# A new table of places for the preparations, and a plan with two transfer queues, in a planned attention and feed-forward kernel

## The chip, the cores and the metric

The kernel runs on one core of a Trainium2 chip. The metric is device microseconds (us) of one execution; lower is better. The kernel before was timed three times: median 1328.38 us, from 1326.26 to 1328.97. A core has five engines with their own instruction streams: PE (matrix products), DVE (VectorE), ACT (ScalarE), POOL (GpSimd) and SP (SyncE, which here only starts transfers).

## The reference

Attention over four batches, with keys that are means over 4 x 4 windows, and behind it a feed-forward layer with the activation h - tanh(h):

```python
kv_pool = kv.reshape(B, H // r, r, W // r, r, C).mean(axis=(2, 4))
k = v = kv_pool.reshape(B, -1, C) @ w_sr           # 768 keys of 128 per batch
a = softmax(q @ k.T / sqrt(C))                     # 12288 queries per batch
x = (a @ v).reshape(B * S, 128)
h = x @ w_in                                       # 128 -> 2048
out = (h - tanh(h)) @ w_out                        # 2048 -> 128
```

## The kernel before, in words

The 49152 queries are cut into 96 units of 512 (24 per batch). The kernel uses that the softmax is nearly flat and that x hardly moves about a centre: it computes exp(s) - 1 - s beside a straight (linear) term, and the feed-forward as a polynomial about the centre. A last part checks that this holds, and a branch that isn't taken here holds the general way.

One unit is, on each engine, a fixed row of work:

- PE: 3 pairs of score products (`scores`, L774), 3 pairs of value products (`values`, L818), 2 products for the softmax's sum (`shares`, L802), 2 x 3 straight products (L808, L878), 8 pairs into the wide layer (`forth`, L889) and 8 pairs back (`back`, L927). A product has 512 columns; a pair fills one of three PSUM tiles named `big`, or adds to the bank `acc`.
- ACT: 3 `exps` (L778), 7 `square` (L893), 1 `copy` (L900), and `result` (L938, tile o) that ends a unit and waits for the unit's last product into acc.
- DVE: 3 `beyond` (L781, tile r2, which `order` prints as r_ and a number), 7 `cube` (L896), 1 `apart` (L829, tile df).
- POOL: one of the eight wide tiles whole: `moved_pool` (L903, z), `times` (L907) twice (z, then rp, which the last product of the unit needs), the roundings `rounded` (L832, dr, from df; all `forth` of the unit need it), `lower_left` (L858, dl) and `lower_q` (L812, ql), and two accumulating transfers `added` (L797) that sum the three r2 tiles into rs for `shares`.
- SP: the transfers of q, of the first r2 tile into rs (`copied`, L794), and of the output.

Before the units of batch 1, 2 and 3, each batch has **preparations**, which run between the units of the batch before it: 15 accumulating transfers `gather` (L366, POOL; the 16th, the first, from SP) that sum the 16 places of a window into kvp; `keys` (L355: six partial sums L428, their mean L432 and L433, the centre L440 on PE, keys L447, values L456, moment L473), and `about_centre` (L504: the centre through the wide layer L536, small polynomial chains on POOL L561 to L592, scaled weights L636, L678, L698 on POOL, slopes L685 on PE). Batch 0's preparations run before the first unit; so do the weights' (`words_of`, `weights`), but for the product W W^T (L333), which only the last check needs.

The order is written by `Plan.run`: every piece of work has a step (its due place), an engine, a length and how late its result is, and the planner takes at each moment the piece that can start first, and among those within 0.1 us the one with the lowest step. The pieces of the units (`lane=True`) keep the order of their steps on each engine, which the table `AT` gives; the preparations are set between them by step. Each engine then runs its instructions in exactly that order, and waits at each for what it needs. A transfer costs the planner the time `dma` on one shared resource.

Of the kernel before, what the change touches and what calls it, by code (L numbers as in the profile page):

```python
# [22 lines left out]
KB = 64  # L23
# [23 lines left out]
class Plan:  # L47

    HOP = 0
    OWN = {"DVE": 0.16, "ACT": 0.02}  # L50
    SOON = 0.1

# [29 lines left out]
    def run(self, between):  # L82
# [25 lines left out]
        free, ready, done, begun, order = {}, {}, [0.0] * n, [0.0] * n, []  # L108
# [3 lines left out]
        while any(ready.values()):  # L112
            best = None
            for e, q in ready.items():
                if q:
# [6 lines left out]
                    if best is None or (start, step, i) < best[:3]:  # L122
                        best = start, step, i, e, r
            now, _, i, e, r = best
            ready[e].remove((r, i))
            step, _, us, _, late, port, dma = self.ops[i]
            free[e] = now + us
            if dma:
# [4 lines left out]
            begun[i], done[i] = now, now + us + late  # L133
            order.append((now, i))
            for k in then[i]:
                left[k] -= 1
                if not left[k]:
                    f = self.ops[k][1]
                    own = self.OWN.get(f, 0.0)
                    r = [done[j] + (self.HOP if self.ops[j][1] != f else own) for j in need[k]]  # L140
                    r = max(r + [begun[j] + 0.01 for j in behind[k]])
                    ready.setdefault(f, []).append((r, k))
# [14 lines left out]
def attention_then_ffn(ctx: ExitStack, tc: tile.TileContext, q, kv_by_key, kv_by_place, w_sr, w_in,  # L157
# [18 lines left out]

    DIRECT, HELD = 2, 6
# [3 lines left out]
            "most": 1}  # L181

# [51 lines left out]
    def words_of(step, load_step, n, kind):  # L234
# [55 lines left out]
        Y, M, part = (ym, "y"), (ym, "m"), (key, n)  # L290
        plan.op(load_step, "SP", 0.5, load_words, () if kind == "i" else ("held",), (words,), late=2.0,
# [13 lines left out]
    def weights(step, load_step):  # L305
# [3 lines left out]
        for j in range(2):  # L309
            turned = f"turned.{j}"  # L310
            big(turned, step + NW + j)
            for k in range(2):
# [6 lines left out]
                plan.op(step + NW + j, "PE", 1.0, turn, (("win32", 2 * j + k), "ident"),  # L319
# [5 lines left out]
            plan.op(step + NW + j, "ACT", 1.03, copy, (turned,), (("winT", j),), late=0.1)  # L325
        s = 16.0
        bank("WW", "x", s)
        sb("WW32", "W2", [P, P])
        bank("W4", "x", s + 1)
# [11 lines left out]
        norm(s + 1, "WW32", "W4", B)  # L341
# [13 lines left out]
    def keys(b, s0):  # L355
# [6 lines left out]
        NK = K // KB  # L362
        for w in range(W if b else 0):
            def gather(w=w):
                if w:
                    PL.dma_start(out=plan[kvp], in_=kv_by_place[b - 1, w], accum_op=ALU.add)  # L366
                else:
                    SP.dma_start(out=plan[kvp], in_=kv_by_place[b - 1, w])

            at = (b * NG - GATHER[b - 1] + max(w - 1, 0)) * UN + AT["more"][0] - 2 * UN  # L370
            plan.op(at - (0.01 if w else 4), *(("POOL", 0.87) if w else ("SP", 0.5)), gather, (), (kvp,),
                    late=3.0, dma=1.0, lane=w > 0)
        for j in range(0 if b else NK):
# [3 lines left out]
            at = slice(j * KB, (j + 1) * KB)  # L377

            def load(at=at, key=key):
                SP.dma_start(out=plan[key], in_=kv_by_key[:, at, :])  # L380

            plan.op(s - 8, "SP", 0.5, load, (), (key,), late=2.0, dma=1.27)
            if j % 3 == 2:
                for k, w in enumerate((8, 4, 2, 1)):
                    def fold(key=key, w=w, at=at):
                        x = plan[key]
                        to = plan[kvp][:, at].unsqueeze(2) if w == 1 else x[:, :, 0:w]
                        PL.tensor_tensor(out=to, in0=x[:, :, 0:w], in1=x[:, :, w : 2 * w], op=ALU.add)
# [3 lines left out]
            else:  # L392
                def pool(key=key, at=at):
                    V.tensor_reduce(out=plan[kvp][:, at], in_=plan[key], op=ALU.add, axis=AX.X)
# [13 lines left out]
        for x, at in ((pc, s0), (pm, s3), (p4, s4)):  # L408
            bank(x, "x", at)
# [74 lines left out]
        for n in range(NK // 2):  # L484
            of = (kvp,) if b else ((kvp, 2 * n), (kvp, 2 * n + 1))
            plan.op(s0 - 0.5, "DVE", 0.3, partial(part, n), of, ((row, n),))
        plan.op(s0, "DVE", 0.35, mean, (row,), (row,))
        plan.op(s0, "ACT", 0.85, apart, (kvp, row), (kvp,), late=0.1)
        plan.op(s0, "PE", 0.2, centre, ("wsr", row), (pc,), late=0.2)
        plan.op(s0, "DVE", 0.12, copy_centre, (pc,), (cen,))  # L490
# [13 lines left out]
    def about_centre(b, s0):  # L504
# [24 lines left out]
        if not b:  # L529
            bank(f"{pa}.0", "acc", slopes_at[0])  # L530
# [697 lines left out]
```

## Time and profile before

| | us |
|---|---|
| median of the timed runs | 1328.38 |
| span of the profiled execution (first to last instruction) | 1326.8 |
| PE busy | 1271.4 (96%) |
| DVE busy | 1220.6 (92%) |
| ACT busy | 1197.4 (90%) |
| POOL busy, without the issuing of transfers | 1143.5 (86%) |

The page gives the profiled execution's span and no other time of it; the span lies inside the range of the timed runs, 1.6 us under their median. Four engines are nearly full, so a share of busy time says little here. What says more is when each unit ends (ACT's L938, 96 times) and which chain of waits runs from one unit to the next.

### The profile page before, as it was taken

To read this page: it belongs to the slowest core of one execution; us is meant where nothing else is said; L and a number is where in the kernel's file an instruction comes from. 1 tells how busy PE (TensorE), PEld (TensorE's weight loads), DVE (VectorE), ACT (ScalarE), POOL (GpSimd) and SP (SyncE) were. 2 spreads that over 40 slices of the span, in tenths; PEclk is the share of its full clock that TensorE was granted. 3 is DMA by queue.
4 is the path that set the end of the run, shared out by engine and by line. 5 is a ranking of instruction groups with operands and counts; after the bars stand their busy time and mean duration, and the time that the engine had idled before them with its cause. 6 is when DMAs were issued, how large, how long until landed. Compare 5 with 4: busy or idle time off the path is not lost.

```text
span 1326.8 us, 17379 instructions
## 1 busy us (share of the span) xinstructions
PE 1271.4 (96%) x5520; PEld 889.0 (67%) x5520; DVE 1220.6 (92%) x1201; ACT 1197.4 (90%) x1423; POOL 1143.5 (86%) x969
## 2 busy tenths in 40 slices
PE   4899999899899999999999999999999999999997
PEld 3666666676666667766666666776767667667665
DVE  6789999788899999999899999999999999899996
ACT  4689999788899999899899999899899999899996
POOL 3587999779999988799999998799998889798896
PEclk8899999999999999999999999999999999999999
DMA  9255666436566654445566664444444444434431
GB/s 350 52 112 128 139 134 141 94 106 129 125 136 140 134 128 97 114 112 132 115 142 133 136 137 110 104 104 112 104 108 107 104 119 96 103 97 108 115 82 40
DMA packets 82708, 158.47 MB, mean 119 GB/s; under 512 B 9936, under 2 KB 12112, under 8 KB 82608
## 3 DMA queue, kind: packets, MB, share of 16 engines
q0 software_dynamic: 33552, 66.99, 30.8%
q1 hardware_dynamic: 49056, 90.29, 19.4%
q8 instruction: 45, 0.74, 0.2%
q14 instruction: 55, 0.45, 0.1%
HBM read 57.93 MB, written 25.39 MB: 63 GB/s over the span
## 4 chain that ended last, share of the span: by engine, by line
POOL 44%; PE 38%; ACT 6%; issue 6%; DMA 2%; DVE 2%; SPq 0%; POOLq 0%; ACTq 0%; DVEq 0%
PE acc L927 11%; POOL rp L907 11%; PE big L889 10%; POOL z L907 10%; POOL rs L797 6%; PE big L774 5%; POOL z L903 4%; PE x L818 4%; POOL ql L812 3%; POOL dr L832 3%; ACT E L778 3%; PE x L808 2%; PE acc L878 2%; ACT v L900 2%; POOL kvp L366 1%
## 5 line engine op out<-in xcount | busy, mean ns | idle before, releaser
L896 DVE SCALAR_TENSOR_TENSOR r<-big,u 128x1024 fp32r<-128x1024 f32 x672 | 778.9, 1217 | 27.9 <-ACT u L893 27.5
L893 ACT ACTIVATE u<-big 128x1024 f32<-128x1024 f32 x672 | 662.4, 1034 | 34.3 <-PE big L889 23.4
L889 PE MATMUL big<-dr,winr 128*128 128x512 f32 x1536 | 510.4, 413 | 1.7 <-DVE r L781 0.9
L927 PE MATMUL acc<-r,Wr 128*128 128x512 f32 x1344 | 426.8, 409 | 0.6 <-DVE r L896 0.6
L781 DVE SCALAR_TENSOR_TENSOR r<-E,big 128x1024 f16<-128x1024 f32 x288 | 350.2, 1217 | 51.1 <-ACT E L778 48.0
L889 PEld LDWEIGHTS big<-dr,winr 128*128 128x128 f32 x1536 | 276.5, 188 | 97.0 <-DVE r L781 25.8
L778 ACT ACTIVATE E<-big 128x1024 f32<-128x1024 f32 x288 | 296.0, 1029 | 19.9 <-PE big L774 9.7
L927 PEld LDWEIGHTS acc<-r,Wr 128*128 128x128 f32 x1344 | 251.8, 188 | 65.1 <-DVE r L896 1.5
L907 POOL TENSOR_TENSOR rp<-z,v 128x1024 fp32r<-128x1024 f32 x96 | 273.5, 2849 | 0.2
L907 POOL TENSOR_TENSOR z<-z,v 128x1024 f32<-128x1024 f32 x96 | 248.7, 2590 | 4.3
L797 POOL DMA_DIRECT2D rs<-r x188 | 223.7, 1190 | 6.9 <-DVE r L896 4.7
L774 PE MATMUL big<-qr,kTr 128*128 128x512 f32 x576 | 198.2, 426 | 4.8 <-ACT qr L759 1.6
L832 POOL TENSOR_SCALAR dr<-df 128x512 fp32r<-128x512 f32 x96 | 69.8, 727 | 122.9 <-DVE df L829 115.4
L818 PE MATMUL x<-r,vvr 128*128 128x512 f16 x576 | 175.2, 387 | 0.0
L812 POOL TENSOR_TENSOR ql<-q,qr 128x512 fp32r<-128x512 f32 x96 | 164.5, 1714 | 6.0 <-ACT qr L759 6.0
L858 POOL TENSOR_TENSOR dl<-df,dr 128x512 fp32r<-128x512 f32 x96 | 164.8, 1716 | 0.0
L774 PEld LDWEIGHTS big<-qr,kTr 128*128 128x128 f32 x576 | 105.9, 191 | 44.7 <-DVE r L781 13.3
L903 POOL TENSOR_SCALAR z<-v 128x1024 f32<-128x1024 f32 x96 | 111.0, 1156 | 0.0
L900 ACT COPY v<-big 128x1024 f32<-128x1024 f32 x96 | 97.7, 1018 | 1.5 <-PE big L889 1.3
L938 ACT ACTIVATE o<-acc,At 128x512 f32<-128x512 f32 x96 | 65.7, 684 | 30.4 <-PE acc L927 29.7
L927 PE MATMUL acc<-rp,Wr 128*128 128x512 f32 x192 | 74.3, 469 | 17.8 <-POOL rp L907 14.6
L818 PEld LDWEIGHTS <-vvr 128*128 128x128 f16 x576 | 33.7, 99 | 79.8 <-issue 79.3
(184 smaller groups left out, 1008.5 us busy)
## 6 DMA issues: line engine op xcount, KB each, us to landing
rs<-r POOLq DMA_DIRECT2D x188, 256.0 KB, 3.9
q<-in_q_dram SPq DMA_DIRECT2D x96, 256.0 KB
out_dram<-o SPq DMA_DIRECT2D x96, 256.0 KB
rs<-r SPq DMA_DIRECT2D x94, 256.0 KB
kvp<-in_kv_by_place_dram POOLq DMA_DIRECT2D x45, 384.0 KB, 4.9
r<-in_kv_by_key_dram SPq DMA_DIRECT2D x6, 512.0 KB
kc<-inverse SPq DMA_DIRECT2D x12, 256.0 KB
u<-in_moe_w_in_dram SPq DMA_DIRECT2D x3, 512.0 KB
```

The source lines that it names most:

```text
L774: PE.matmul(out=half(plan[s], h), lhsT=plan[kTr][:, n * P : (n + 1) * P], rhs=plan[qr], start=True, stop=True)
L778: A.activation(out=plan[e], in_=plan[s], func=AF.Exp)
L781: V.scalar_tensor_tensor(out=plan[r], in0=plan[e], scalar=-1.0, in1=plan[s], op0=ALU.add, op1=ALU.subtract)
L797: PL.dma_start(out=plan[rs], in_=plan[r2s[k]], accum_op=ALU.add)
L812: PL.tensor_tensor(out=plan[ql], in0=plan[qs], in1=plan[qr].bitcast(F32), op=ALU.subtract)
L818: PE.matmul(out=plan[num], lhsT=plan[vvr][:, n], rhs=half(plan[f"r2.{g}.{k}"], h), start=(start and h == 0), stop=(stop and h == 1))
L858: PL.tensor_tensor(out=plan[dl], in0=plan[df], in1=plan[dr].bitcast(F32), op=ALU.subtract)
L889: PE.matmul(out=half(plan[hp], h), lhsT=plan[winr][:, f * P : (f + 1) * P], rhs=plan[dr], start=True, stop=True)
L893: A.activation(out=plan[u], in_=plan[hp], func=AF.Square)
L896: V.scalar_tensor_tensor(out=plan[r], in0=plan[hp], scalar=1.0, in1=plan[u], op0=ALU.add, op1=ALU.mult)
L907: PL.tensor_tensor(out=plan[to], in0=plan[x], in1=plan[y], op=ALU.mult)
L927: PE.matmul(out=plan[acc], lhsT=plan[Wr][:, 2 * n + h], rhs=half(plan[r], h), start=(start and h == 0), stop=(stop and h == 1))
```

## The change

Three things change; no computation does.

The planner's model of transfers: instead of one shared resource there are two queues (SP's and POOL's), each in order, which share the transfer engines half and half when both are active. Lengths and latencies of several pieces are set anew (`added` 0.87 to 0.9 us, `apart` 0.6 to 0.685 us, and so on), and the `HOP` between engines, which was 0, is gone.

All places of the units' work (`AT`) are other numbers, and `num`, the place of a PSUM bank, has its own.

A table `MOVES` gives single pieces of the preparations a shift of their step, through `at(step, name, ...)`: gathers, partial sums, centres, keys, slopes, scaled weights, and the product W W^T (`WW`, by -172.2).

```diff
-    HOP = 0
+    AHEAD = {"SP": 0.72, "POOL": 0.3}
+    QUEUES = ("SP", "POOL")
...
+        def landed(until):
+            nonlocal clock
+            while any(queue.values()):
+                active = [e for e in self.QUEUES if queue[e] and queue[e][0][0] <= clock]
+                rate = 1.0 / max(1, len(active))
...
-                free["dma"] = max(free.get("dma", 0.0), now + us) + dma
-                late += free["dma"] - (now + us)
...
+                queue[e].append([now + us + self.AHEAD[e], dma, i])
...
+    MOVES = {
+        "load.i.0": -22.9, "load.i.1": -18.7, "words.i.1": -54.5, "words.i.3": -7.3, "WW": -172.2,
...
+    def at(step, *name):
+        return step + MOVES.get(".".join(str(x) for x in name), 0.0)
...
-            at = (b * NG - GATHER[b - 1] + max(w - 1, 0)) * UN + AT["more"][0] - 2 * UN
-            plan.op(at - (0.01 if w else 4), *(("POOL", 0.87) if w else ("SP", 0.5)), gather, (), (kvp,),
-                    late=3.0, dma=1.0, lane=w > 0)
+            put = at((b * NG - GATHER[b - 1] + max(w - 1, 0)) * UN - 17.0, "gather", c, w)
+            plan.op(put - (0.01 if w else 4), *(("POOL", 0.88) if w else ("SP", 0.5)), gather, (), (kvp,),
+                    late=0.81 if w else 1.0, dma=2.3 if w else 1.1)
...
-        more=[6.92, 9.07],
...
+        more=[-2.2, -1.7], num=-5.0, copied=16.8, added=[-26.1, -22.4], shares=-5.6, left=-8.4,
```

Line numbers after the change are about 76 higher from `Plan.run` on (L907 is L983, L797 is L873, L366 is L437, L428 is L502).

How instructions move, first on POOL, in a unit of batch 0 that holds a gather (the row named kvp). Before:

```order
L832 TENSOR_SCALAR dr<-df 128x512
L903 TENSOR_SCALAR z<-v 128x1024
L366 DMA kvp<-in_kv_by_place_dram 128x768
L907 TENSOR_TENSOR z<-z,v 128x1024
L797 DMA rs<-r_1416 128x1024
L907 TENSOR_TENSOR rp<-z,v 128x1024
L858 TENSOR_TENSOR dl<-df,dr 128x512
L812 TENSOR_TENSOR ql<-q,qr 128x512
L797 DMA rs<-r_1451 128x1024
```

And after, in one of the four units of batch 0 that hold two gathers:

```order
L979 TENSOR_SCALAR z<-v 128x1024
L908 TENSOR_SCALAR dr<-df 128x512
L983 TENSOR_TENSOR z<-z,v 128x1024
L437 DMA kvp<-in_kv_by_place_dram 128x768
L873 DMA rs<-r_908 128x1024
L983 TENSOR_TENSOR rp<-z,v 128x1024
L934 TENSOR_TENSOR dl<-df,dr 128x512
L437 DMA kvp<-in_kv_by_place_dram 128x768
L873 DMA rs<-r_888 128x1024
L888 TENSOR_TENSOR ql<-q,qr 128x512
```

In every unit the first z now stands before dr, and ql behind the second accumulation. The gathers of batch 1 are through after seven units, where they took thirteen; those of batches 2 and 3 stand mostly one to a unit, between ql and z.

On DVE, the six partial sums of batch 1's keys (row<-kvp), the mean behind them and the centre (col). Before:

```order
L829 TENSOR_TENSOR df<-x,t 128x512
L781 SCALAR_TENSOR_TENSOR r_2267<-E,big 128x1024
L896 SCALAR_TENSOR_TENSOR r<-big,u 128x1024 x5
L428 TENSOR_REDUCE row<-kvp 128x4 x6
L896 SCALAR_TENSOR_TENSOR r<-big,u 128x1024
L432 TENSOR_REDUCE row<-row 128x1
L433 TENSOR_SCALAR row<-row 128x1
L896 SCALAR_TENSOR_TENSOR r<-big,u 128x1024
L443 TENSOR_SCALAR col<-x 128x1
```

After (four of the six have been done in the two units before):

```order
L905 TENSOR_TENSOR df<-x,t 128x512
L502 TENSOR_REDUCE row<-kvp 128x4 x2
L857 SCALAR_TENSOR_TENSOR r_1879<-E,big 128x1024
L506 TENSOR_REDUCE row<-row 128x1
L507 TENSOR_SCALAR row<-row 128x1
L972 SCALAR_TENSOR_TENSOR r<-big,u 128x1024
L517 TENSOR_SCALAR col<-x 128x1
L972 SCALAR_TENSOR_TENSOR r<-big,u 128x1024 x2
```

The six sums stood in one block; they are spread over three units, and PE's centre product (L440, now L514), which stood before the straight products at the unit's end, stands between two `back` pairs.

On PE, the product W W^T stood in the second unit, and now stands behind the first sixteen products of the program. Before, around it:

```order
L889 MATMUL big<-dr,winr 128x512 x2
L927 MATMUL acc<-r,Wr 128x512 x2
L333 MATMUL x<-winT 128x128 x16
L927 MATMUL acc<-r,Wr 128x512 x2
L889 MATMUL big<-dr,winr 128x512 x2
```

After, from the program's start:

```order
L384 MATMUL big<-ident,win_67 128x128 x16
L403 MATMUL x<-winT 128x128 x16
L488 MATMUL big<-kvp,ident 128x512 x4
L514 MATMUL x<-row,wsr 128x1
L488 MATMUL big<-kvp,ident 128x512
```

It moved ahead of all units, to where PE has only batch 0's preparations.

## Rows read from the trace of the kernel before

**Rows 1.** ACT's timeline, `result` of nine units: start, length, instruction, idle before.

```profile
100.79 0.68 ACT L938 ACTIVATE o<-acc,At 128x512 f32<-128x512 f32 x1
...
226.43 0.69 ACT L938 ACTIVATE o<-acc,At 128x512 f32<-128x512 f32 x1 [0.24 <-PE acc L927]
...
376.06 0.69 ACT L938 ACTIVATE o<-acc,At 128x512 f32<-128x512 f32 x1 [0.69 <-PE acc L927]
...
501.54 0.68 ACT L938 ACTIVATE o<-acc,At 128x512 f32<-128x512 f32 x1
...
653.82 0.69 ACT L938 ACTIVATE o<-acc,At 128x512 f32<-128x512 f32 x1 [1.05 <-PE acc L927]
...
816.99 0.68 ACT L938 ACTIVATE o<-acc,At 128x512 f32<-128x512 f32 x1
...
967.25 0.69 ACT L938 ACTIVATE o<-acc,At 128x512 f32<-128x512 f32 x1 [0.23 <-PE acc L927]
...
1113.92 0.68 ACT L938 ACTIVATE o<-acc,At 128x512 f32<-128x512 f32 x1
...
1156.34 0.68 ACT L938 ACTIVATE o<-acc,At 128x512 f32<-128x512 f32 x1
```

**Rows 2.** Busy in one unit: length, PE, PEld, DVE, ACT, POOL, clock.

```profile
1009.00:1021.20 12.20, 12.20 (x53) 8.54 (x52) 12.13 (x12) 11.95 (x15) 10.62 (x9) 1.00 0.44 108
```

**Rows 3.** Timelines of POOL, ACT, DVE in one unit with a gather.

```profile
169.38 2.69 POOL L907 TENSOR_TENSOR z<-z,v 128x1024 f32<-128x1024 f32 x1
...
172.34 3.01 POOL L907 TENSOR_TENSOR rp<-z,v 128x1024 fp32r<-128x1024 f32 x1
...
176.17 0.69 ACT L938 ACTIVATE o<-acc,At 128x512 f32<-128x512 f32 x1 [0.25 <-PE acc L927]
...
178.95 0.68 DVE L829 TENSOR_TENSOR df<-x,t 128x512 f32<-128x512 f32 x1
...
179.73 0.62 POOL L832 TENSOR_SCALAR dr<-df 128x512 fp32r<-128x512 f32 x1 [1.07 <-DVE df L829]
...
181.33 0.86 POOL L366 DMA_DIRECT2D kvp<-in_kv_by_place_dram  x1
181.95 2.71 POOL L907 TENSOR_TENSOR z<-z,v 128x1024 f32<-128x1024 f32 x1
```

**Rows 4.** Timeline of POOL in one unit without gather.

```profile
1023.81 0.87 POOL L797 DMA_DIRECT2D rs<-r  x1
...
1028.07 1.54 POOL L812 TENSOR_TENSOR ql<-q,qr 128x512 fp32r<-128x512 f32 x1
1029.31 1.14 POOL L797 DMA_DIRECT2D rs<-r  x1
1031.91 0.61 POOL L832 TENSOR_SCALAR dr<-df 128x512 fp32r<-128x512 f32 x1 [1.46 <-DVE df L829]
```

**Rows 5.** Timeline of PE, the product W W^T in the second unit.

```profile
90.03 3.73 PE L333 MATMUL x<-winT 128*128 128x128 f32 x32
```

**Rows 6.** Timeline of PE, the centre of batch 1's keys.

```profile
239.50 0.35 PE L440 MATMUL x<-row,wsr 128*128 128x1 f32 x2 [2.97 <-DVE row L433]
```

**Rows 7.** The chain that ended last: PE's pieces of keys and slopes.

```profile
39.95 1.60 PE x L473 x12
...
57.04 1.79 PE acc L685 x16
...
251.77 0.64 PE big L447 x2
...
261.51 0.67 PE big L456 x6
262.18 0.79 PE x L536 x8
```

**Rows 8.** From issue to landing: transfers into rs, then POOL's gathers.

```profile
DMA to landing us min/median/max: 3.3/3.9/6.5
...
DMA to landing us min/median/max: 4.5/4.9/6.1
```

More of the change, by code (lines that the diff above doesn't have):

```diff
@@ L107, in run, with release, finish @@
                 then[k].append(i)
[L108 removed]
+        free, ready, begun, order = {}, {}, [0.0] * n, []
+        since = [0.0] * n
+        queue = {e: [] for e in self.QUEUES}
+        clock = 0.0
+        def release(k):
+            left[k] -= 1
+            if not left[k]:
+                ready.setdefault(self.ops[k][1], []).append((since[k], k))
+        def finish(i, at):
+            e = self.ops[i][1]
+            for k in then[i]:
+                if i in need[k]:
+                    f = self.ops[k][1]
+                    r = at + (self.OWN.get(f, 0.0) if f == e else 0.0)
+                    if f == "POOL" and self.ops[k][6]:
+                        r += self.BEGIN
+                    since[k] = max(since[k], r)
+                    release(k)
+        def landed(until):
[3 more added lines that the diff above has]
+                rate = 1.0 / max(1, len(active))
+                at, e = min((clock + queue[e][0][1] / rate if e in active else queue[e][0][0],
+                             self.QUEUES.index(e)) for e in self.QUEUES if queue[e])
+                to = min(at, until)
+                if to > clock:
+                    for x in active:
+                        queue[x][0][1] -= rate * (to - clock)
+                    clock = to
+                if at > until:
+                    return None
+                if self.QUEUES[e] in active:
+                    return queue[self.QUEUES[e]].pop(0)[2]
+            return None
         for i in range(n):
@@ L123, in run @@
                         best = start, step, i, e, r
+            done = landed(best[0] if best else math.inf)
+            if done is not None:
+                finish(done, clock + self.ops[done][4])
+                continue
+            if best is None:
+                break
             now, _, i, e, r = best
+            if not any(queue.values()):
+                clock = max(clock, now)
             ready[e].remove((r, i))
@@ L127, in run @@
             free[e] = now + us
-            if dma:
-                free["dma"] = max(free.get("dma", 0.0), now + us) + dma
-                late += free["dma"] - (now + us)
             if port:
                 free["port"] = now + us
-            begun[i], done[i] = now, now + us + late
+            begun[i] = now
             order.append((now, i))
             for k in then[i]:
[L136 to L142, printed above, removed]
+                if i not in need[k]:
+                    since[k] = max(since[k], now + 0.01)
+                    release(k)
+            if dma:
+                queue[e].append([now + us + self.AHEAD[e], dma, i])
+            else:
+                finish(i, now + us + late)
         assert len(order) == n, "the plan has a cycle"
```

143 lines of the change are left out of this document (77 added, 66 removed), and 16 rows, old and new, of the table MOVES.

## The prediction

> **What bounds the kernel now.** I read the ends of the units first, because shares of busy time are near full on four engines and separate nothing. The differences of the nine rows of `result` (units 1, 11, 21, 31, 42, 55, 66, 78 and 81) give the mean unit of each stretch [rows 1]: units 1 to 11, 12.56 us; 11 to 21, 14.96; 21 to 31, 12.55; 31 to 42, 13.84; 42 to 55, 12.55; 55 to 66, 13.66; 66 to 78, 12.22; 78 to 81, 14.14. So there are three kinds of stretch: a plain unit of 12.2, a unit of 12.55 where POOL also issues one gather, and three stretches of 10 or 11 units where the preparations of batch 1, 2 and 3 run (the three units at 78 hold the early part of the last check).
>
> Then one plain unit by engines: 12.20 us, of which PE is busy 12.20, DVE 12.13, ACT 11.95, POOL 10.62 [rows 2]. PE has no gap there: 12.2 is its own work, and nothing that only moves work gets below it. POOL waits 1.46 us for df before dr [rows 4].
>
> Then a unit with a gather, step by step [rows 3]. From z (169.38) to the start of rp (172.34) 2.96 us; rp lasts 3.01 and ends at 175.35; the pair of products that needs it takes until o at 176.17 (0.82); behind o on ACT and DVE stand an exp and its r2 tile, and df starts 2.78 later (178.95); dr 0.78 later (179.73); then dr itself, the first z and the gather's issue until the next wide z at 181.95: 2.22. The sum is 12.57, and that is the unit: a loop through POOL, PE, ACT and DVE whose every step waits for the one before, with the gather's issue inside it. Without the gather the loop is shorter than PE's 12.2, and PE decides.
>
> In the preparations of batch 1 the waits are plain to see: PE stands 2.97 us at the centre's product for the mean on DVE [rows 6], since six partial sums stand there in one block.
>
> **The change part by part.** It removes and adds no arithmetic, so I count, stretch by stretch, the time above 12.22 a unit, and what of it the new places can give back. The sum is made against the profiled span of 1326.8, which lies 1.6 us under the median of the timed runs; differences are taken over as they are.
>
> *Units with a gather* (10 + 10 + 13 = 33 units). They lie 125.6 + 125.5 + 163.2 - 33 x 12.22 = 11.0 us above plain ones [rows 1]. In the new order the first z stands before dr, so dr is followed by the wide z at once (dr lasts 0.62), and most gathers stand between ql and that first z. The same loop is then 2.96 + 3.01 + 0.82 + 2.78 + 0.78 + 0.6 = 10.95 us, 1.25 under PE's unit; a gather's issue of 0.62 (181.33 to 181.95) lies in POOL's spare 1.46 [rows 3, 4]. So the 11.0 us can go whole. Against it: four units now hold two gathers each, and there the second accumulation stands close behind a gather in the same queue. Each could wait some 1 to 2 us, which takes back up to 8, of which POOL's spare time covers the first part; I take back 4. Value -7, bounds -11 and 0.
>
> *W W^T*. It took PE 3.73 us inside the second unit [rows 5], with nothing beside it that could have kept PE's time. It now stands before the keys of batch 0, where PE waits for transfers. Value -3.7; if it holds up the centre behind it there, the gain falls to 0.
>
> *Preparations of batch 1* (units 11 to 21). They lie 149.6 - 10 x 12.22 = 27.4 us above plain ones [rows 1]. PE's own share of this: four pieces L536 at 0.79 = 3.2, two L447 at 0.64 = 1.3, two L456 at 0.67 = 1.3, L473 1.6, sixteen slope products L685 at twice 1.79 for 32 records = 3.6 [rows 7]; together 11.0. That must stay, so at most 16.4 can go. The lower bound is nothing. The nearest rows are those of batches 2 and 3, the same work with its partial sums already in three pieces: 152.3 - 134.4 = 17.9 and 150.3 - 134.4 = 15.9 above plain [rows 1]. The new places split the six sums over three units and set the centre between two `back` pairs, so PE has work where it stood; I take batch 1 to the level of batch 2: 27.4 - 17.9 = 9.5. Value -9.5, bounds -16 and 0.
>
> *Preparations of batches 2 and 3*: 17.9 + 15.9 = 33.8 above, 22.0 of it PE's own work. At most 11.8 can go. POOL's pieces are now mostly one to a unit, where 1.46 us are spare, but in each of the two batches one chain of small operations stands between dr and rp, inside the loop. I take -3, bounds -12 and +6 (each of about six misplaced pieces a microsecond).
>
> *The last check's early part* (units 78 to 81): 42.4 - 36.7 = 5.8 above plain [rows 1]. Its thirteen POOL operations stood between the first z and the wide z, in the loop; they now stand before the first z. Value -3, bounds -5 and 0.
>
> *Plain units.* PE's work is the same. DVE has only 0.07 us a unit to spare and ACT 0.25 [rows 2], and the new order of the three r2 tiles among the seven wide ones is not in the trace. If it costs 0.05 us in each of some 60 units that is 3; the other bound is nothing, since PE has no gap to give. I take +2.
>
> *The start before the first result.* The order there changes little, except that four gathers stand before the first units instead of two. 0, bounds -3 and +4.
>
> Sum: -7 - 3.7 - 9.5 - 3 - 3 + 2 = -24.2. The median 1328.4 becomes 1304. With most terms at half or at one and a half of their value, this case reaches from 1293 to 1317.
>
> One rule of the Trainium skill speaks against pairing the gathers. POOL's second accumulation waits until the first has landed, 3.9 us after its issue in the middle [rows 8]; it was issued 5.5 us behind the first (1023.81 to 1029.31), and without ql between them (1.24) that is 4.26 [rows 4], so 0.36 us are left. The page "DMA: Bandwidth & Descriptors" (section "Issuing engines are not separate DMA queues") says that transfers started by different engines run on the same 16 transfer engines and interleave, so that a gather beside an accumulation delays both. The same page's fit (section "Anatomy of one DMA") of 2.0 us and bytes / 436e3 would make 2.6 us of 256 KB, an estimate by which 1.7 us would be left; the row's 3.9 is longer, and decides.
>
> **The rivals.**
>
> *PE's work is already the floor.* The preparations' excess is largely products (33 of 61 us), and smoothing shifts it only. Then the gather's 7 and W W^T's 3.7 come, and nothing else: 1328.4 - 10.7 = 1318. For it: batches 2 and 3 lie only 5 to 7 us above their own products. Against it: batch 1 lies 16 above them, with a wait of 2.97 in one place [rows 6].
>
> *The second accumulation waits for the first in every unit* (slower). Place: POOL, L797, for rs. POOL can lose 1.46 us a unit before PE feels it [rows 4], so this decides once a landing takes more than 4.26 + 1.46 = 5.7 us; the longest in the trace took 6.5, the shortest 3.3 [rows 8]. If landings were 6.3 throughout, each of 94 units would be 0.6 longer: +56 - 24, 1360; at 6.0 it is +28 - 24, 1332. For it: the new order has cut the distance by a quarter. Against it: the middle value is 3.9 beside gathers too.
>
> *The new order of plain units is itself longer.* With 0.07 us to spare on DVE, 0.25 us more in each of 95 units takes all 24 back: 1328. For it: nothing in the trace shows the new order. Against it: the same work in the old order runs at PE's own pace, and the loop through POOL became shorter by 1 us and more.
>
> *More goes than I count*: if nearly all that isn't PE's work goes (11 + 3.7 + 16 + 12 + 5 = 48, less a few), 1285.
>
> **How the numbers follow.** A measurement of this kernel tells 0.2%, some 2.7 us, from no change. My case (1293 to 1317) has 0.60; PE as the floor (about 1318, to 1325) 0.15; more (under 1293) 0.06; the plain units' order eating the gain 0.06; the waiting accumulation 0.13, all of it slower but for the part near 1330. Faster: 0.60 + 0.15 + 0.06 = 0.81; same 0.06; slower 0.13. The range from 1290 to 1328 leaves out about 0.04 below and 0.15 above. Predicted 1304.
>
> **What would show it.** In the changed kernel's trace units with one gather should end 12.2 us apart, not 12.55; L403 (W W^T) should run before 30 us, and the second unit lose its 4 us; PE should have no gap over 1 us at L514 for batch 1; units with two gathers may take 13. The prediction is wrong if plain units take over 12.3, if POOL's rows show waits for rs on landings, or if the stretches of batches 2 and 3 grow above 14 a unit.

## The result and the profile after

The changed kernel takes 1289.96 us (median of 4 runs, 1289.32 to 1293.98), the kernel before beside it 1327.32 (1325.3 to 1328.97): ratio 0.9728, 95% interval 0.9711 to 0.9745. That is 37 us, where 24 were forecast. The profiled execution took 1289.32 us with a span of 1287.6.

The ends of the same nine units on ACT's timeline, which answer to [rows 1]:

```profile
90.99 0.68 ACT L1014 ACTIVATE o<-acc,At 128x512 f32<-128x512 f32 x1
...
221.38 0.68 ACT L1014 ACTIVATE o<-acc,At 128x512 f32<-128x512 f32 x1
...
351.99 0.68 ACT L1014 ACTIVATE o<-acc,At 128x512 f32<-128x512 f32 x1
...
477.16 0.68 ACT L1014 ACTIVATE o<-acc,At 128x512 f32<-128x512 f32 x1
...
621.22 0.68 ACT L1014 ACTIVATE o<-acc,At 128x512 f32<-128x512 f32 x1
...
784.89 0.69 ACT L1014 ACTIVATE o<-acc,At 128x512 f32<-128x512 f32 x1
...
929.06 0.68 ACT L1014 ACTIVATE o<-acc,At 128x512 f32<-128x512 f32 x1
...
1078.04 0.68 ACT L1014 ACTIVATE o<-acc,At 128x512 f32<-128x512 f32 x1
...
1116.21 0.68 ACT L1014 ACTIVATE o<-acc,At 128x512 f32<-128x512 f32 x1
```

Differences of such rows give the length of each stretch. A single unit is named here, and in the expectations, by the result that it follows: unit 2 runs from result 2 to result 3. The first table sets the two kernels beside those experiments that start from the changed kernel; the experiments' names are explained below.

```
stretch (units)  before   after  no_moves  winr   start  single  pairs
first result      84.26   78.75   83.89   78.42   78.80   77.97  80.86
0 to 1            16.53   12.24   15.90   15.91   12.25   12.25  12.25
1 to 11          125.64  130.39  123.78  123.59  123.10  146.90 128.11
11 to 21         149.63  130.61  149.43  149.60  149.70  131.09 130.59
21 to 31         125.48  125.17  124.01  123.99  124.03  126.11 124.99
31 to 42         152.28  144.06  156.04  153.94  155.22  144.05 144.07
42 to 55         163.17  163.67  160.82  160.85  161.15  163.78 164.13
55 to 66         150.26  144.17  154.70  154.99  154.15  144.12 144.06
66 to 78         146.67  148.98  147.46  147.44  147.50  148.98 148.98
78 to 81          42.42   38.17   38.15   38.18   38.15   38.17  38.14
81 to 92         134.01  134.59  134.59  134.57  134.56  134.64 134.59
```

Before to after: 5.5 us come from the start, 4.3 from W W^T, 14.3 from units 1 to 21, 11.8 from units 21 to 78, 4.3 from the last check; 0.8 go back behind unit 81, in the plain units and the end. That is 39.4, against 39.2 between the two spans. Preparations now run in other units than before, so units 1 to 21 are read together.

One plain unit by engines, as in [rows 2] (length; busy time on PE, PEld, DVE, ACT, POOL; then clock, DMA share, GB/s):

```profile
986.00:998.29 12.29, 12.29 (x54) 8.50 (x53) 12.10 (x12) 12.10 (x15) 10.64 (x9) 1.00 0.43 108
```

The chain that ended last, by engine, before and then after:

```profile
POOL 44%; PE 38%; ACT 6%; issue 6%; DMA 2%; DVE 2%; SPq 0%; POOLq 0%; ACTq 0%; DVEq 0%
```

```profile
PE 74%; POOL 14%; DMA 4%; issue 2%; DVE 2%; ACT 2%; SPq 0%; POOLq 0%; ACTq 0%; DVEq 0%
```

From unit 1 to unit 66 PE's idle time has almost gone; in units 11 to 21 before, PE was busy 138.74 of 149.63:

```profile
90.99:929.06 838.07, 834.44 (x3665) 584.39 (x3664) 801.20 (x777) 800.55 (x946) 785.32 (x664) 1.00 0.55 126
```

That leaves 3.6 us of idle time in 838. It isn't all that PE loses, for its busy time is not a fixed amount, as the part on the prediction shows.

A unit with one gather, on POOL, which answers to [rows 3]:

```profile
402.61 1.92 POOL L888 TENSOR_TENSOR ql<-q,qr 128x512 fp32r<-128x512 f32 x1
403.85 1.52 POOL L437 DMA_DIRECT2D kvp<-in_kv_by_place_dram  x1
404.83 1.64 POOL L979 TENSOR_SCALAR z<-v 128x1024 f32<-128x1024 f32 x1
405.84 1.20 POOL L908 TENSOR_SCALAR dr<-df 128x512 fp32r<-128x512 f32 x1
406.55 2.87 POOL L983 TENSOR_TENSOR z<-z,v 128x1024 f32<-128x1024 f32 x1
```

ql, the gather and the first z fill the time in which POOL used to wait for df; dr doesn't wait, and 0.71 us behind its start the wide z begins. In [rows 3] that distance was 2.22. The unit around these rows is 12.29 long, not the 12.2 of the forecast.

Where two gathers stand in one unit the next rows of POOL show the forecast price, in brackets:

```profile
110.54 1.22 POOL L437 DMA_DIRECT2D kvp<-in_kv_by_place_dram  x1
111.16 1.50 POOL L873 DMA_DIRECT2D rs<-r  x1
...
115.71 1.47 POOL L437 DMA_DIRECT2D kvp<-in_kv_by_place_dram  x1
117.79 0.85 POOL L873 DMA_DIRECT2D rs<-r  x1 [0.61 <-DMA rs<-r]
...
131.44 0.86 POOL L873 DMA_DIRECT2D rs<-r  x1 [1.24 <-DMA rs<-r]
```

The second accumulation waits for the first one's landing; a fourth such wait, of 1.04 us, follows at 151.92. The five units 2 to 6 take 12.44, 13.02, 13.63, 13.44 and 12.47 us, 3.6 above five plain ones of 12.29.

On PE, W W^T (L403) and the centre of batch 1 (L514), for [rows 5, 6]; neither has an idle time behind it in brackets:

```profile
15.29 3.74 PE L403 MATMUL x<-winT 128*128 128x128 f32 x32
...
187.00 0.28 PE L514 MATMUL x<-row,wsr 128*128 128x1 f32 x2
```

### The profile page after: what moved, and what is told of

The parts are those of the page before. It is cut to its first block, busy times and chain, and to the rows that moved or that the text cites. A ratio compares the mean times of both kernels' runs of the same rounds, so it can differ in the third digit from the quotient of the medians.

```text
span 1287.6 us, 17375 instructions
## 1 busy us (share of the span) xinstructions
PE 1257.1 (98%) x5520; PEld 879.8 (68%) x5520; DVE 1213.7 (94%) x1201; ACT 1201.0 (93%) x1423; POOL 1147.5 (89%) x969
## 4 chain that ended last, share of the span: by engine, by line
PE 74%; POOL 14%; DMA 4%; issue 2%; DVE 2%; ACT 2%; SPq 0%; POOLq 0%; ACTq 0%; DVEq 0%
PE big L965 23%; PE acc L1003 22%; PE big L850 8%; PE x L894 8%; PE acc L954 4%; PE x L884 4%; DMA rs<-r 3%; POOL rp L983 3%; PE x L878 3%; POOL z L983 2%; POOL z L979 2%; POOL rs L873 2%; POOL ql L888 1%; POOL dl L934 1%; DVE r L972 1%
## 5 line engine op out<-in xcount | busy, mean ns | idle before, releaser
L972 DVE SCALAR_TENSOR_TENSOR r<-big,u 128x1024 fp32r<-128x1024 f32 x672 | 788.7, 1218 | 26.8 <-ACT u L969 26.4
L969 ACT ACTIVATE u<-big 128x1024 f32<-128x1024 f32 x672 | 671.1, 1029 | 34.8 <-PE big L965 23.3
L965 PE MATMUL big<-dr,winr 128*128 128x512 f32 x1536 | 518.9, 419 | 0.7 <-DVE r L972 0.6
L1003 PE MATMUL acc<-r,Wr 128*128 128x512 f32 x1344 | 414.5, 398 | 0.6 <-DVE r L972 0.6
L983 POOL TENSOR_TENSOR rp<-z,v 128x1024 fp32r<-128x1024 f32 x96 | 270.8, 2821 | 0.2
L983 POOL TENSOR_TENSOR z<-z,v 128x1024 f32<-128x1024 f32 x96 | 243.8, 2539 | 0.1
L873 POOL DMA_DIRECT2D rs<-r x188 | 211.2, 1124 | 7.6 <-DMA rs<-r 6.1
L979 POOL TENSOR_SCALAR z<-v 128x1024 f32<-128x1024 f32 x96 | 122.7, 1278 | 82.1 <-ACT v L976 81.8
L850 PE MATMUL big<-qr,kTr 128*128 128x512 f32 x576 | 193.0, 417 | 0.4 <-ACT winr L746 0.2
L888 POOL TENSOR_TENSOR ql<-q,qr 128x512 fp32r<-128x512 f32 x96 | 185.2, 1929 | 1.1 <-ACT qr L835 1.1
L908 POOL TENSOR_SCALAR dr<-df 128x512 fp32r<-128x512 f32 x96 | 81.4, 848 | 0.0
```

What stands on the lines that cost most here:

```text
L850: PE.matmul(out=half(plan[s], h), lhsT=plan[kTr][:, n * P : (n + 1) * P], rhs=plan[qr], start=True, stop=True)
L873: PL.dma_start(out=plan[rs], in_=plan[r2s[k]], accum_op=ALU.add)
L888: PL.tensor_tensor(out=plan[ql], in0=plan[qs], in1=plan[qr].bitcast(F32), op=ALU.subtract)
L965: PE.matmul(out=half(plan[hp], h), lhsT=plan[winr][:, f * P : (f + 1) * P], rhs=plan[dr], start=True, stop=True)
L969: A.activation(out=plan[u], in_=plan[hp], func=AF.Square)
L972: V.scalar_tensor_tensor(out=plan[r], in0=plan[hp], scalar=1.0, in1=plan[u], op0=ALU.add, op1=ALU.mult)
```

## The experiments

### The loop of the gather units: z moved, gather moved, gather made small

All three start from the kernel before and alter the finished order of its instructions; the third also cuts the bytes of the gathers.

**z ahead of dr** (1314.29 us, ratio 0.9898, 0.9883 to 0.9913):

```
 order.sort()
+# each z on POOL: one place up, over the dr that stands directly ahead
+if name.get(line[last]) == "dr" and ...: line.insert(last, line.pop(here))
```

> The kernel before with one other thing altered in the finished order: z of a unit (1.07 us on POOL) stands ahead of dr instead of behind it; the gather stays between dr and the first product. Theory (loop): the loop of the gather units loses z, 12.57 - 1.07 = 11.5 us, less than PE's 12.2, so the gather units come to 12.2 to 12.3 as if the gather had been moved: ratio 0.992 to 0.994; plain units are unchanged at 12.22, because PE sets them. Rival (the gather costs its time wherever it stands): no change, ratio 1.000. Second rival (z ahead of dr delays dr, since z waits for v, and df is then read late): plain units lengthen, ratio above 1.002.

```profile
176.32 1.05 POOL L911 TENSOR_SCALAR z<-v 128x1024 f32<-128x1024 f32 x1 [0.72 <-ACT v L908]
176.53 0.47 SPq L802 DMA_DIRECT2D rs<-r  x1
177.34 0.61 POOL L840 TENSOR_SCALAR dr<-df 128x512 fp32r<-128x512 f32 x1
177.91 0.88 POOL L374 DMA_DIRECT2D kvp<-in_kv_by_place_dram  x1
...
180.90 1.19 POOL L805 DMA_DIRECT2D rs<-r  x1
```

(The row on SPq is SP's copy into rs.) The gather still stands in the loop (177.91), and yet the 33 gather units fall from a mean of 12.55 to 12.25 (122.55 + 122.37 + 159.49 over 33), most of them to 12.20 to 12.27; plain units stay at 12.22. So the loop is what set them: taking z out of it is enough. Of the 13 us, 9.9 are these units; 1.9 come at the last check and 0.8 ahead of the first result, which the forecast ratio of 0.992 to 0.994 didn't count. The theory holds, and both rivals fall.

**The gather ahead of dr** (1352.89 us, ratio 1.0185, 1.0172 to 1.0199):

```
 order.sort()
+# each gather on POOL: up over z and dr, directly ahead of dr
+if to and ...: line.insert(to[-1], line.pop(here))
```

> The kernel before with one thing altered in the finished order: a gather that POOL issued behind dr and z now stands directly ahead of dr, in the time in which POOL waits for df. Everything else stands where it stood; on the queue the gather keeps its place between the second accumulation of one unit and the first of the next. Theory (loop): in gather units POOL's dr, z, gather, product and the way back to dr form a loop of 12.57 us; without the gather it is shorter than the 12.2 us of PE's work, so the 33 gather units come down to 12.2 to 12.3: -8 to -11 us, ratio 0.992 to 0.994. Rival (the gather costs its time on POOL, or its transfer slows the accumulations, wherever it stands): gather units stay at 12.5, ratio 1.000.

I was wrong here, and neither the theory nor the rival gave this time: these units became 13.3 us long, not 12.2 and not 12.5. The rival's second half, that the gather's transfer slows the accumulations, is what the rows show, but not "wherever it stands". POOL's timeline, and the copy on SP's queue between:

```profile
166.48 1.17 POOL L806 DMA_DIRECT2D rs<-r  x1
167.07 1.48 POOL L375 DMA_DIRECT2D kvp<-in_kv_by_place_dram  x1
...
168.03 0.47 SPq L803 DMA_DIRECT2D rs<-r  x1
...
168.70 0.62 POOL L841 TENSOR_SCALAR dr<-df 128x512 fp32r<-128x512 f32 x1
...
174.48 0.89 POOL L806 DMA_DIRECT2D rs<-r  x1 [1.63 <-DMA rs<-r]
```

The gather no longer delays dr (no bracket at 168.70), so the loop did get shorter. But it was now issued 1 us ahead of SP's copy (168.03), which starts the tile rs of the next accumulation, and 0.59 us behind an accumulation (166.48). POOL's first accumulation then waited 1.63 us for a landing in rs, 6.45 us behind the copy's issue. In the run above the copy is issued 1.4 us ahead of the gather and the accumulation comes 4.4 us behind it, without a wait.

**The same order with small gathers** (1318.46 us, ratio 0.9936, 0.9921 to 0.9951):

```
-PL.dma_start(out=plan[kvp], in_=kv_by_place[b - 1, w], ...)
+PL.dma_start(out=plan[kvp][:, 0:96], in_=kv_by_place[b - 1, w, :, 0:96], ...)
```

> The kernel before with the gather directly ahead of dr, which took 1352.9 us, and with each gather of POOL cut to the first 96 of its 768 columns, 48 KB instead of 384 KB; so the other columns of the pooled keys and values of batches 1 to 3 are left out. The order on every engine and both queues is that of the slow kernel. Theory (SP's copy into rs was issued 1 us behind the gather there and landed late because the gather's bytes shared the engines with it; POOL's next first accumulation waited 1.6 to 1.8 us for it): with an eighth of the bytes the copy lands in time, gather units come from 13.4 to 12.2 us, ratio 0.990 to 0.993 to the kernel before. Rival (the place in POOL's order itself costs the time: dr comes later by the gather's issue): gather units stay at 13.3 to 13.5, ratio 1.018.

```profile
172.80 1.46 POOL L375 DMA_DIRECT2D kvp<-in_kv_by_place_dram  x1
...
174.17 0.47 SPq L803 DMA_DIRECT2D rs<-r  x1
...
178.92 0.88 POOL L806 DMA_DIRECT2D rs<-r  x1
```

Same order, an eighth of the bytes, and the wait is gone: 4.75 us behind the copy the accumulation starts without one, and the gather units stand at 12.25 in the mean. So the place in POOL's order costs nothing by itself; the gather's bytes, in that place, do. The two runs' landings of the gather itself, first 384 KB, then 48 KB, from the view of the tile kvp:

```profile
DMA to landing us min/median/max: 6.7/6.7/6.8
```

```profile
DMA to landing us min/median/max: 4.2/4.2/4.2
```

The rule that the prediction took from the Trainium skill ("DMA: Bandwidth & Descriptors", section "Issuing engines are not separate DMA queues") says that transfers of different engines interleave on the same transfer engines. These runs agree, for a copy on SP's queue against a gather on POOL's: the wait of 1.63 us comes with the bytes and goes with them, and its price is 1.0 us a unit (13.29 against 12.25).

Which place is a bad one these runs settle only in part. In those units of the changed kernel that hold one gather, it often stands ahead of the copy too (by up to 2.1 us), and no accumulation waits. One such place, where unit 16 begins (length 13.14):

```profile
286.96 1.56 POOL L873 DMA_DIRECT2D rs<-r  x1
...
288.81 1.89 POOL L437 DMA_DIRECT2D kvp<-in_kv_by_place_dram  x1
...
290.01 0.47 SPq L870 DMA_DIRECT2D rs<-r  x1
...
295.67 0.93 POOL L873 DMA_DIRECT2D rs<-r  x1
```

The gather is 1.2 us ahead of the copy here, and the accumulation 5.66 us behind the copy has no wait. One thing that differs is that ql stands between the accumulation ahead and the gather (1.85 us between their starts, 0.59 in the slow run). No run alters that distance alone.

### What the planner, the unit's order and the moves do apart

**The planner's model alone** (1346.44 us, ratio 1.0142, 1.012 to 1.0164): the changed kernel with the old step numbers of a unit and without moves. Its gathers, as in the changed kernel, have no fixed place among POOL's other instructions.

```
-MOVES = {"load.i.0": -22.9, ...
+MOVES = {}
...
-AT = dict(forth=[4.5, 6.4, ...
+AT = dict(forth=[3.94, 1.06, ...
```

> The changed kernel's planner (two queues that share the engines, the new costs), with the unit's step numbers of the kernel before, the gathers at their old steps without a fixed place among POOL's other instructions, and an empty table of moves. POOL then issues the gather directly ahead of dr in 28 of the 33 gather units, as in the run that took 1352.9 us. Theory (a gather in front of SP's copy delays it, whoever lists it there): these units at 13.2 to 13.6 us, the other stretches as before, ratio 1.010 to 1.018. Rival (the new model lists copy and gather so that they do not meet): gather units at 12.2 to 12.3, ratio 0.990 to 0.993.

```profile
166.49 1.49 POOL L420 DMA_DIRECT2D kvp<-in_kv_by_place_dram  x1
...
174.13 0.89 POOL L858 DMA_DIRECT2D rs<-r  x1 [1.85 <-DMA rs<-r]
```

The planner that knows of two queues sharing the engines put the gather ahead of dr by itself, and ran into the same wait; its 33 gather units have a mean of 13.29, as in the run with the moved gather. The new model, then, is no gain of its own; it needs the new step numbers of a unit, by which most gathers stand behind ql. The other stretches were not "as before", as I had expected: units 11 to 21 took 144.48 us for 149.63, and the first result came at 81.66 for 84.26.

**Everything but the moves** (`no_moves`, 1327.35 us, ratio 0.9997, 0.9987 to 1.0006):

```
-MOVES = {"load.i.0": -22.9, ...}
+MOVES = {}
```

> The changed kernel with an empty table of moves: the planner's new model, the new step numbers of a unit and the gathers' new place stay, every piece of the preparations goes back to its old step. Theory (the places of the pieces are a part of their own): the gather units fall from 12.55 to about 12.3 us, plain units stay at the changed kernel's 12.29, W W^T comes back into PE's path (first stretch between two results 16.5 us), the stall of batch 1's preparations (27.4 us above plain units, of which PE's own work is 11) and the 5.8 us of the last check stay; the time is about 1327 - 8 + 4 = 1323 us, ratio 0.993 to 1.000. Rival (the new order of a unit, with z and ql ahead of dr, has room enough for the pieces wherever they stand): two thirds or more of the 37 us are already here, time at or under 1302 us, ratio at or under 0.981. On the first result: if it comes at 78.7 us here too, the unit's order or the model made the start shorter; if at about 84.3, the moved places of batch 0 did.

The gather units come down (units 1 to 11, 21 to 31, 42 to 55 in the table) and so does the last check; the preparations of batches 2 and 3 get worse by 3.8 and 4.4, and the sum is nothing. Unit 15, in batch 1's preparations, takes 25.75 us. PE and POOL there:

```profile
298.71 2.29 POOL L739 TENSOR_TENSOR Wg<-winT,hb 128x512 f32<-128x512 f32 x2
...
300.07 2.09 PE L746 MATMUL x<-Wg,wout 128*128 128x129 f32 x8 [8.99 <-POOL Wg L739]
```

PE works its instructions off in their listed order, and a slope product stood 9 us ahead of the Wg that POOL, busy with its own unit and six small operations, had yet to make. All of PE's unit waited behind it. One unit each of batches 2 and 3 (20.48 and 21.26 us) holds the same wait for Wg, of 4.8 and 5.4 us; in the changed kernel the like units take 13.1. The rival (room enough in the new order) falls: given the new order of a unit, without the moves nothing of the 37 us is left, because these three units take back what the order gives.

**Only the moves of the start** (`start`, 1317.12 us, ratio 0.9924, 0.991 to 0.9937):

```
-MOVES = {..., "keys.0.1": -23.6, "first.1.0": -33.4, ...}
+MOVES = {those of the weights, W W^T and batch 0}
```

> The changed kernel with only the moves that concern the start (the weights, batch 0's pieces, W W^T); the moves of batches 1 to 3 are taken out, which is the kernel with the empty table plus the start. Theory (the start's 5.5 us and W W^T are made by these moves and kept to the end): first result at 78.7 instead of 83.9 us, the stretch between the first two results 12.3 instead of 15.9, all later stretches as with the empty table: 1327.4 - 5.2 - 3.6 = 1318.6 us, ratio 0.993 to 0.994. Rival (an earlier start is given back, because the loads and the gathers of batch 1 come no earlier): the stretches after it take up what the start gained, ratio 0.997 to 1.000.

The first result comes at 78.80, and 12.25 us lie between the first two; next to nothing is given back in the stretches that follow. These moves are worth 10 us, the moves of batches 1 to 3 the other 27.

**winr alone** (`winr`, 1320.15 us, ratio 0.9945, 0.9924 to 0.9965):

```
+MOVES = {"winr.0": 30.5}
```

> The changed kernel with one single move in the table, batch 0's winr by 30.5 (PE's products that scale the first weights stand behind the first score products, not ahead of them); W W^T, batch 0's other pieces and batches 1 to 3 are as with the empty table, whose first result is at 83.9 us and whose time is 1327.4. Theory (the start is shorter because the first scores come first): first result near 79 us, later stretches as with the empty table, 1323 us, ratio 0.996 to 0.997. Rival (it needs the moves together, the loads of the weights too): first result at 82.5 us or later, ratio 0.998 or above.

PE's order around the first score products (L833, L835; L721 and L723 scale the first weights), without the move and with it:

```profile
40.30 2.84 PE L721 MATMUL big<-Wg,winT 128*128 128x128 f32 x24
42.89 0.71 PE L833 MATMUL big<-qr,kTr 128*128 128x512 f32 x2
```

```profile
37.84 1.17 PE L835 MATMUL big<-qr,kTr 128*128 128x512 f32 x4
...
41.86 2.94 PE L723 MATMUL big<-Wg,winT 128*128 128x128 f32 x24 [0.81 <-DVE r L842]
```

One move makes the whole gain of the start: 78.42 for the first result. The scores, which ACT and DVE wait for, come 5 us earlier, and the weights are still ready in time.

**W W^T alone, in the kernel before** (1324.87 us, ratio 0.9978, 0.9968 to 0.9987):

```
-s = 16.0
+s = 16.0 - 172.2
...
-bank("W4", "x", s + 1)
+bank("W4", "x", s + 11.9)
...
-norm(s + 1, "WW32", "W4", B)
+norm(s + 11.9, "WW32", "W4", B)
```

> The kernel before with W W^T alone set to the step that the change gives it, so that PE makes it while it waits for the first loads; the pieces around it in the prologue shift by a few places, since the planner lists anew. Theory (W W^T was on the path of PE between the first two results): that stretch falls from 16.5 to about 12.3 us, first result unchanged at about 84.3 us, -3.7 to -4.3 us, ratio 0.997. Rival (what is left out there is paid ahead of the first result, since ACT's copy and DVE's norm of it now stand in the prologue's path): first result 3 to 4 us later, ratio 1.000. If the first result comes earlier by 4 us or more, this is what made the start of the changed kernel shorter.

The stretch between the first two results falls from 16.53 to 12.57, as expected. The first result comes at 82.96, not later. The whole time fell by 2.5 us; its interval (1.7 to 4.2) still holds the 4.0 of the stretch.

### Batch 1: the pairs of gathers and the block of partial sums

**Single gathers** (`single`, 1306.4 us, ratio 0.9842, 0.9829 to 0.9856):

```
-    "gather.1.7": -25.8, "gather.1.9": -32.0, "gather.1.11": -45.4, "gather.1.13": -60.7,
-    "gather.1.15": -59.9, ...
```

> The changed kernel without the five moves of batch 1's gathers: POOL then issues one gather a unit over ten units and two in one, where the changed kernel issues two a unit in units 2 to 6. The other pieces keep their places. Theory (two gathers in a unit make the second accumulation wait, POOL loses 0.6 to 1.2 us there and the units take 13.0 to 13.6 us): units 3 to 6 come down to 12.3 to 12.5, the ten units from the first to the eleventh result from 130.4 to about 127, 3 us off the time, 1286 us, ratio to the kernel before 0.970. Rival (batch 1's last gathers now land when its pieces want kvp, and these wait instead): units 10 to 17 longer by the same 3 us or more, ratio 0.973 or above.

```profile
DVE row L499 <- DMA kvp<-in_kv_by_place_dram: 13.1, 1, 13.1
POOL kvp L434 <- DMA kvp<-in_kv_by_place_dram: 4.2, 1, 4.2
```

Both happened: units 3 to 6 fell to 12.28 and 12.29, and unit 8 grew to 33.75, as DVE waited 13.1 us for the last gather with all its other work behind. The rival's mechanism was right and its size far too small. With the other pieces where the moves set them, the pairs cost 3.6 us and save 20 (unit 8 takes 13.35 with them).

**The pairs set differently** (`pairs`, 1289.05 us, ratio 0.971, 0.9691 to 0.9728):

```
 order.sort()
+# a gather directly ahead of an accumulation: directly behind it (and behind ql)
+if name.get(line[pool[0]]) == "added":
+    ...
+    line.insert(to, line.pop(here))
```

> The changed kernel with one thing altered in the finished order: in the units with two gathers, the one that POOL issued directly ahead of a unit's first accumulation is issued directly behind it, and the one directly ahead of the second accumulation behind it and ql, which is how the paired units of batches 2 and 3 already stand. Theory (a gather ahead of an accumulation on POOL's queue delays its landing, and the accumulation behind waits for that on POOL): units 2 to 6 come from 12.44, 13.02, 13.63, 13.44, 12.47 to 12.3 to 12.7 each, about 2 to 3 us in all; everything behind stays; 1287 us, ratio to the kernel before 0.969 to 0.971, and no wait of an accumulation for a landing over 0.3 us in these units. Rival (two gathers a unit load the engines whatever their place): units 2 to 6 as they are, ratio 0.973.

```profile
112.39 0.86 POOL L883 DMA_DIRECT2D rs<-r  x1
...
117.52 1.22 POOL L883 DMA_DIRECT2D rs<-r  x1
```

The accumulations of these units have no wait left, and units 2 to 6 take 12.30, 12.33, 12.45, 13.15 and 12.48: 2.3 us less, as expected. In the unit of 13.15, above the range that I gave, a gather waits 0.74 us on POOL for the landing of the one before. In the whole time this can't be told from the changed kernel (0.9728, 0.9711 to 0.9745), the more since the first result came 2.1 us later in the profiled run; the gathers ahead of the first units were moved by the same edit.

**The partial sums back in one block** (1294.52 us, ratio 0.9739, 0.9718 to 0.976):

```
 order.sort()
+# the six sums of batch 1, directly ahead of their mean
+order = [(begun[i], i) for i in line[:to] + sums + line[to:]]
```

> The changed kernel with one thing altered in the finished order: the six partial sums of batch 1's pooled rows, which DVE makes in four different units, stand in one block directly ahead of their mean, as in the kernel before. Theory of the prediction (the block, 1.25 us on DVE with the mean and PE's centre behind it, is what made PE wait 2.97 us there and its clock fall): the unit with the mean, 13.17 to 13.91 us, becomes 2 to 4 us longer, ratio 0.975 to 0.976. Rival (what cost the time was the heap of pieces behind the block, first sums, centre, first weights and norms in one unit; the block alone is taken by DVE's slack): that unit at most 1 us longer, ratio 0.973.

```profile
190.50 0.38 PE L519 MATMUL x<-row,wsr 128*128 128x1 f32 x2 [0.37 <-DVE row L512]
```

PE waits 0.37 us at the centre, not 2.97, and the unit goes from 13.35 to 14.44. (In the changed kernel the sums stand in three units, not in four as I wrote: 156.82 to 184.31.) The block costs about 1 us, so my reason for batch 1's gain falls. The other 2.2 us by which units 1 to 11 were longer in this profile lie in the paired units ahead of the block, whose order the edit doesn't touch; why they took longer stays open.

### The parts put together otherwise

**The old unit with z first, the new planner and moves** (1314.04 us, ratio 0.9896, 0.988 to 0.9911):

```
 order.sort()
+# each z on POOL ahead of dr, each gather behind dr
...
-"gather.1.7": -25.8, "gather.1.9": -32.0, ...
-AT = dict(forth=[4.5, 6.4, ...
+AT = dict(forth=[3.94, 1.06, ...
```

> A version put together from the parts: the changed kernel's planner and its moves (without those of gathers), with the unit's step numbers of the kernel before, z ahead of dr, and single gathers behind dr, as in the run that took 1314.3 us. Theory (the parts add: 12.22 us for plain and gather units in place of 12.29 and up to 13.6, with the start and the pieces of the changed kernel): 1289.3 - 0.07 x 55 - 8 for units 1 to 11 - 3 for batch 2's and 3's gather units = about 1275 to 1281 us, ratio 0.960 to 0.965. Rival (the places were found for the other order of a unit and do not fit this one): first and plain units as said, but stretches with preparations longer by 1 us a unit or more, time 1290 to 1310, ratio 0.972 to 0.987.

```profile
PE x L525 <- DVE row L518: 11.5, 1, 11.5
```

Plain and gather units do run at 12.20 to 12.25. But one unit of 28.83 holds this wait of PE, as with single gathers, the first result comes at 85.81, and the last check's three units take 41.97. The whole time lies above the rival's range too; without that unit's 16.6 us above a plain one it would be some 1297, within it. The parts don't add, and the rival's reading, that the places belong to the order they were found for, fits this, but no run tries it apart. No run here beats the changed kernel by more than can be measured.

## Why the prediction fell short

The way of the change was forecast. The range, from 1290, holds the measured 1289.96 only at its very edge (as a ratio to the kernel before, the range began at 0.971, and 0.9728 was measured). That it did is partly luck: my own case ended at 1293, and less than that had a chance of 0.06. The sum of 24.2 was 13 us too small for the timed runs and 15 for the two spans. Step by step:

- **Gather units.** Loop and price were right: without z, or without z and the gather, in the loop these units stand at PE's pace (12.25 in the run with z moved; 12.29 after, where the new unit sets it). What I missed is that the place of the gather in POOL's order isn't free: close behind an accumulation and 1 us ahead of SP's copy it made these units 13.29, 0.7 more than before.
- **Paired gathers.** I took back 4 us for four units; 3.6 in five were measured, with the mechanism named there: waits of 0.61 to 1.24 us for the first accumulation's landing. So one of the signs named for a wrong forecast, waits for rs on landings, did show, in these units. The rival that this wait comes in every unit fell: on the whole trace POOL waits 6.1 us, in 8 places, for landings in rs.
- **W W^T.** -3.7 forecast, -4.3 measured, and -4.0 in the run that moves it alone.
- **The start.** "The order there changes little" was the step that failed. PE's products that scale the first weights moved behind the first scores, and that alone is 5.5 us where I gave 0 and a bound of -3.
- **Batch 1.** For units 1 to 21 the sum says -3.4 + 4 - 9.5 = -8.9; -14.3 was measured. I took batch 1 only to the level of batches 2 and 3, and I laid the waits to the block of sums, which is worth 1 us. A larger part, 10 of the 27.4 us above plain units, stands elsewhere in the trace before. From result 16 to result 21 POOL is busy the whole time, PE waits 4.8 us for rp, and five units take 71.06 us, where five plain ones take 61.1 (PE's own products for batch 1 are a part of the rest):

```profile
305.00:376.06 71.06, 65.31 (x287) 45.92 (x286) 61.52 (x59) 61.53 (x74) 71.06 (x59) 1.00 0.60 129
```

- **Batch 1 after.** These five units take 63.13 us. POOL is busy as long over units 1 to 21 as before (244.8 us for 244.3), but some 5 us of it now lie in units 1 to 11. PE waits 2.4 us in units 1 to 11, all of it in the paired units, and not at all in units 11 to 21. Without the moves PE waited 9 us for one Wg. That the moves gain by setting each product of PE behind the piece of POOL it needs is my reading; no run moves batch 1's pieces one by one.
- **Batches 2 and 3.** -3.3 - 4.3 - 3 = -10.6 for units 21 to 78, -11.8 measured. The terms are right only as a sum, since preparations moved into the gather units: units 21 to 31 and 42 to 55 are within 0.5 us of before.
- **The last check.** -3 forecast, -4.3 measured; the order of a unit gives it, since the run without moves has it too.
- **Plain units.** 0.05 us each forecast, 0.07 measured (12.29 for 12.22, PE full in both); the run with the old unit order has 12.22 again. Where PE loses these 0.07 us I did not find.
- **PE as the floor** was the right bound and the wrong size: the rival left 11 us above PE's work, and 39 went. Nor is PE's busy time the fixed amount that it was taken for. It fell from 1271.4 to 1257.1 us, with 5520 records in both. Some 8 of these 14 us are the gather units, where PE is busy about 12.47 of 12.56 us for 53 records that take 12.20 in a plain unit, at a clock of 1.00 in both; the run with z moved has 1263.1. The rival of 1285 ("more goes") was near, with a chance of 0.06; I had halved most terms without a row that asked for it.
- **PE's clock** has no term in the sum. PE's wait of 2.97 us in [rows 6] and one of 0.75 behind it are followed by 3.5 us in which the granted clock is 0.51, the lower of its two levels (1.2 and 2.4 GHz); it is 1.00 ahead of them and again from 244.51:

```profile
241.00:244.50 3.50, 3.50 (x10) 2.23 (x9) 0.67 (x1) 1.02 (x1) 0.43 (x1) 0.51 0.43 75
```

Behind the 9 us of the run without moves it is 0.50 from 300 to 304. So such a wait costs more than its own length: two L774 products take 1.06 us inside this row and 0.73 from 244.27 on. From unit 1 to unit 92 every unit of the changed kernel has 1.00. In units 78 to 81 PE's busy time fell from 39.62 to 38.17 us with 169 records in both, at clocks of 0.96 and 1.00; how much of the whole gain is the clock's no run separates.

## What to carry to other kernels

Where several engines run nearly full, find the loop whose length is the unit, and take one step out of it. Here z did it, and so did the gather once its bytes were cut; moved whole, the transfer delayed another one from its new place. An instruction listed too early on an engine that works its list off in order stops all that stands behind it (9 us on PE, 13.1 on DVE here), so a piece of preparation belongs behind the time at which its operand is there, not where there is a gap. An excess above an engine's own work that a change sets out to spread should be counted whole, and halved only where a row shows what keeps the rest.

## What had not been expected of the hardware

A gather of 384 KB on POOL's queue, issued 0.59 us behind an accumulation and 1 us ahead of a 256 KB copy on SP's, kept the accumulation behind that copy waiting until 6.45 us after the copy's issue; 48 KB instead, and 4.75 us were enough without a wait. The gather's own landing went from 6.7 to 4.2 us. In the changed kernel a whole gather 1.2 us ahead of the copy, but 1.85 behind the accumulation, left no wait 5.66 us behind the copy.
